# A fifth block product as seven small ones in a mixer's first channel product, with a new order of issue

## The chip, the cores and the metric

The kernel runs on one core of a Trainium2 chip, as one program in one launch. The metric is the device time of that program in microseconds (us); lower is better. Five engines work side by side, each through its own queue in order: TensorE (PE) multiplies, VectorE (DVE) and ScalarE (ACT) do elementwise work, GpSimd (POOL) does a little, and SyncE (SP) issues most transfers. They wait for each other on semaphores. TensorE writes into PSUM[...]; VectorE and ScalarE read those and write SBUF.

## The reference: routed attention, then a token and channel mixer

Four batches of 768 tokens, 512 features, float32:

```
attn = softmax(mask(q k^T / 8)) v                  # 8 heads of 64, keys of the query's cluster only
x    = attn, heads side by side                    # (4, 768, 512)
u    = x + (relu(x^T w_tok1) w_tok2)^T             # token mixing, hidden width 256
out  = u + relu(u w_ch1) w_ch2                     # channel mixing, hidden width 1536
```

The change is in `relu(u w_ch1)`, the first channel product: per batch 768 x 512 times 512 x 1536.

## The kernel before, in words

**Stages.** Attention runs first, then the token mixing of batches 0 and 1 and of 2 and 3, then the channel mixing of batches 0, 2, 3, 1 in that order. Each batch has three parts, so the channel stage has 12. A part makes 512 of the 1536 hidden columns (`ch1_pair`, L784) and uses it at once in the second product (`ch2_chunks`, L960), which adds into the batch's tile `x`.

**Seven products instead of eight.** Both channel products split each operand into 2 x 2 blocks and use Winograd's form of Strassen's scheme: seven block products of sums of blocks, named in `SEVEN` (L545): p1 = A11 B11, p5 = S1 T1, c11 = A12 B21, u2 = S2 T2, c12 = S4 B22, c22 = S3 T3, c21 = A22 T4. The S are sums of weight blocks (the left side), the T sums of blocks of `u` (the right side). A left block of a part is 256 x 256, a right one 256 x 384.

**A second level.** In the first part of batch 0 (`ch1_plain`, L831) all seven are computed as they are, in two chunks of 384 columns each, two matmuls a chunk ("big" products). In the other eleven (`ch1_sets`, L864) four of them, called Y (A12 B21), P (S1 T1), Z (S4 B22) and X (A22 T4), are split once more in the same way, into seven "small" products of 128 x 128 by 128 x 192 each. The rest, A11 B11, S2 T2 and S3 T3, stay big. The left sums of the second level are in the tile `w1ss` (`set_lefts`, L604) and are made once, in batch 0; the right ones, `uTss` (`set_rights`, L620), are made anew for each batch.

**Gathering results.** A small product lies in PSUM, and VectorE adds it (`add`, L566) to the target in SBUF, or ScalarE copies the first one there. Where several partial results accumulate in one bank, the next product may only start when the last state has been read: `chain` (L880) does a small product and the add that reads it. S3 T3 is accumulated in PSUM onto A11 B11 + S2 T2 and VectorE reads the two chunks into `a22`. In the end the hidden blocks pass relu (L810) and VectorE makes the sums S1 to S4 of the second product's left side (L814, L563, L822).

**What sets the order.** The program is written out by hand; no scheduler moves anything. The order of the calls is the order in each queue. Two lists put work between products: `late` holds the rest of a part's gathering and `others` holds weight and right sums; `between` (L740) takes one of each after a big product and after each of the 21 chunks of the second product (`by_turns`, L746). The second product starts with p1, which reads the first hidden block, and reads A12 with c11, in its seventh chunk. In the last part of a batch ScalarE and transfers also turn the next batch's u (`u_steps`, L713), and the right sums for it follow in the first part of the next batch.

**Memory.** The x of batch 1 is written to DRAM after token mixing (`spill`) and read back when batch 0 has left its tile. The tiles for the channel stage reuse the memory of the token stage.

Of the kernel before, what the change touches and what calls it, by code (L numbers as in the profile page):

```python
# [8 lines left out]
F32 = mybir.dt.float32  # L9
# [8 lines left out]
B, H, S, D = 4, 8, 768, 64  # L18
C = 16
# [31 lines left out]
def kernel(  # L51
# [49 lines left out]
    tokpool = pool("tokpool", 1, tokens)  # L101
    staging = fast.enter_context(ExitStack())
# [30 lines left out]
    spill = spilled.tile([P, NJ, DM], F32, name="spill")  # L133
    xs = [(x1pool if b == 1 else xpool).tile([P, NJ, DM], F32, name=f"x{b}") for b in range(B)]
# [466 lines left out]

    def set_lefts():
        if "l2" not in pools:
            pools["l2"] = pools["w2sums"].tile([P, 4, 3, HS], F32, name="w1ss")  # L604
        l2 = pools["l2"]
        yx = W["ch1"].rearrange("p f (i r c) -> p f i r c", i=2, r=2)[:, 2:4]
        pz = pools["w1s"][:, 0:3:2].rearrange("p i f (r c) -> p f i r c", r=2)
        for n, both in enumerate((yx, pz)):
            blocks = [both[:, f, :, r] for r in range(2) for f in range(2)]
            sums_ = [l2[:, 2 * n : 2 * n + 2, m] for m in range(3)]  # L610
            yield dict(
                zip(("A11", "A12", "A21", "A22", "S1", "S2", "S4", "S3"), blocks + sums_ + blocks[2:3])
            )
# [6 lines left out]
    def set_rights():  # L620
        uT, R, r2 = pools["uT"], pools["R"], pools["r2"]
        yz = uT[:, :, 2:4].rearrange("p n f (k t) -> p n f k t", k=2)
        x, p = (R[name].rearrange("p f (k t) -> p f k t", k=2) for name in ("T4", "T1"))
        for blocks, sums_ in (
            ([yz[:, :, f, k] for f in range(2) for k in range(2)], [r2[:, 0:2, m] for m in range(3)]),
            ([x[:, f, k] for f in range(2) for k in range(2)], [r2[:, 2, m] for m in range(3)]),
            ([p[:, f, k] for f in range(2) for k in range(2)], [r2[:, 3, m] for m in range(3)]),
        ):
            yield dict(
                zip(("B11", "B12", "B21", "B22", "T1", "T2", "T4", "T3"), blocks + sums_ + blocks[1:2])  # L630
            )

    def set_right_sums():

        pools["r2"] = pools["w2sums"].tile([P, 4, 3, HS // 2], F32, name="uTss")
        return [list(winograd_right(blocks)) for blocks in set_rights()]

    def set_blocks():

        (yx, pz), (yz, x, p) = (list(y) for y in (set_lefts(), set_rights()))  # L640
        left = {name: {k: a[:, i] for k, a in two.items()} for two, i, name in
                ((yx, 0, "Y"), (yx, 1, "X"), (pz, 0, "P"), (pz, 1, "Z"))}
        right = {"Y": {k: b[:, 0] for k, b in yz.items()}, "Z": {k: b[:, 1] for k, b in yz.items()},
                 "X": x, "P": p}
        return left, right
# [100 lines left out]
    def by_turns(n, product, of, last=False, after=()):  # L746
# [10 lines left out]
        for m in range(len(order) // 2):  # L757
# [9 lines left out]
            between()  # L767
# [16 lines left out]
    def ch1_pair(part, sets, beside):  # L784
# [6 lines left out]
        p5, c12 = (pools["mlp"].tile([P, 2, HS], F32, name=k) for k in ("p5", "c12"))  # L791
# [10 lines left out]

        def big(psum, a, r, i, start):
            product(psum, a, r, i, start)
            between()
            if a != "A11" and beside:
                beside.pop(0)()
# [13 lines left out]
        def sums_34():  # L821
            nc.vector.scalar_tensor_tensor(  # L822
                out=h2["S3"], in0=c12, scalar=0.0, in1=a11, op0=ALU.max, op1=ALU.subtract
            )
            sub(h2["S4"], a12, h2["S2"])

        (ch1_sets if sets else ch1_plain)(
            part, product, big, relu, a11, a12, a22, p5, c12, sum_1, sum_2, sums_34
        )

    def ch1_plain(part, product, big, relu, a11, a12, a22, p5, c12, sum_1, sum_2, sums_34):  # L831
# [24 lines left out]
        def late_(i):  # L856
            product(X[i], "A22", "T4", i, False)
            nc.scalar.activation(out=a12[:, i], in_=X[i], func=ACT.Relu)
            (sums_34 if i else sum_2)()
# [4 lines left out]
    def ch1_sets(part, product, big, relu, a11, a12, a22, p5, c12, sum_1, sum_2, sums_34):  # L864

        left, right = set_blocks()
        n0, n1 = slice(0, HS // 2), slice(HS // 2, HS)

# [7 lines left out]
        def direct(bank, which, start=True):  # L876
            small(bank[:, n0], which, "c11", start)
            small(bank[:, n1], which, "c12", start)

        def chain(q, which, name, x):  # L880

            small(q[:, n0], which, name, name == "p1")
            src = q[:, n0]
            if len(x.shape) == 3:
                src = src.unsqueeze(1).to_broadcast([P, 2, HS // 2])
            add(x, src, x)

        def column(z, which, x):
            small(z[:, n0], which, "p5")
            add(x[:, :, n1], z[:, n0].unsqueeze(1).to_broadcast([P, 2, HS // 2]), x[:, :, n1])  # L890

        X = [ptile("X", HS), None]
        big(X[0], "A11", "B11", 0, True)
        nc.scalar.copy(out=a11[:, 0], in_=X[0])  # L894
        ybe = ptile("Y", HS)
        direct(ybe, "Y")
        add(a11[:, 0], ybe, a11[:, 0])
        X[1] = ptile("X", HS)
        big(X[1], "A11", "B11", 1, True)
        nc.scalar.copy(out=a11[:, 1], in_=X[1])  # L900
        pbe = ptile("Z", HS)
        direct(pbe, "P")
        nc.scalar.copy(out=p5[:, 0], in_=pbe)
        yq, pq = ptile("Y", HS), ptile("Z", HS)
        chain(yq, "Y", "p1", a11[:, 0, n0])
        chain(pq, "P", "p1", p5[:, 0, n0])
        big(X[0], "S2", "T2", 0, False)
        chain(yq, "Y", "u2", a11[:, 0, n1])
        yz, pz = ptile("X", HS), ptile("Z", HS)
        column(yz, "Y", a11)  # L910
        chain(pq, "P", "u2", p5[:, 0, n1])
        small(pz[:, n0], "P", "p5")
        nc.scalar.copy(out=p5[:, 1, n1], in_=pz[:, n0])
        relu(a11[:, 0])
        add(p5[:, 0, n1], pz[:, n0], p5[:, 0, n1])
        add(c12[:, 0], X[0], p5[:, 0])
        big(X[1], "S2", "T2", 1, False)
        chain(yq, "Y", "c22", a11[:, 1, n1])
        chain(pq, "P", "c22", p5[:, 1, n1])
        direct(ybe, "Z")  # L920
        chain(yq, "Y", "c21", a11[:, 1, n0])
        small(pq[:, n0], "P", "c21", False)
        nc.scalar.copy(out=p5[:, 1, n0], in_=pq[:, n0])
        relu(a11[:, 1])
        add(c12[:, 0], ybe, c12[:, 0])
        chain(yz, "Z", "p1", c12[:, 0, n0])
        add(c12[:, 1], X[1], p5[:, 1])
        big(X[0], "S3", "T3", 0, False)
        add(a22[:, 0], X[0], p5[:, 0])
        relu(a22[:, 0])  # L930
        chain(yz, "Z", "u2", c12[:, 0, n1])
        column(pbe, "Z", c12)
        big(X[1], "S3", "T3", 1, False)
        add(a22[:, 1], X[1], p5[:, 1])
        relu(a22[:, 1])
        chain(yz, "Z", "c22", c12[:, 1, n1])
        direct(X[0], "X", False)
        nc.scalar.copy(out=a12[:, 0], in_=X[0])
        small(X[1][:, n0], "X", "c21", False)
        nc.scalar.copy(out=a12[:, 1], in_=X[1])  # L940
        chain(yz, "Z", "c21", c12[:, 1, n0])
        chain(yq, "X", "p1", a12[:, 0, n0])
        sum_1()

        def late_1():
            chain(yq, "X", "u2", a12[:, 0, n1])
            column(pz, "X", a12)
            sum_2()

        def late_2():  # L950
            chain(yq, "X", "c22", a12[:, 1].rearrange("p (k t) -> p k t", k=2))
            relu(a12)
            sums_34()

        late.extend([late_1, late_2])
# [166 lines left out]
    for b in (0, 2):  # L1122
# [26 lines left out]
        if b == 2:  # L1149
            take(turning, len(turning))  # L1150
            usums = u_sums()
            tok2_chunks(b, {13: lambda: next(usums)})
        else:
# [3 lines left out]
            nc.sync.dma_start(spill, xs[1])  # L1157
# [7 lines left out]
    batches = (0, 2, 3, 1)  # L1165
    for n, b in enumerate(batches):
        turning = []
        for part in range(3):
# [8 lines left out]
            ch1_pair(part, not first, [turning.pop(0) for _ in turning[:UCOLS]])  # L1177
# [10 lines left out]
            if part == 2 and not last:  # L1188
                after[3] = lambda: take(turning, len(turning))
# [13 lines left out]
            if part == 2 and not last:  # L1203

                yz, x, p = steps
                yz[0]()
                yz[1]()
                next(usums)

                others += [lambda: next(usums)] * 2  # L1210
                others.append(lambda: [step() for step in (yz[2], p[2], yz[3], p[3])])
                others += [lambda: None, lambda: (x[0](), x[1]()), lambda: (x[2](), x[3]())]
                if n == 0:
                    xs[1] = xpool.tile([P, NJ, DM], F32, name="x0")
                    nc.sync.dma_start(xs[1], spill)
# [216 lines left out]
```

## Time and profile before

Three timed runs gave 823.44 us (823.30 to 823.72). The profiled execution has a span of 821.6 us at a granted TensorE clock of 1.00.

| what | where | us |
|---|---|---|
| channel stage, first product to end | 393.5 to 821.6 | 428 |
| part 0 of batch 0 (all big) | 393.51 to 429.75 | 36.24 |
| part 1 of batch 0 | 429.75 to 465.33 | 35.58 |
| part 2 of batch 0 | 465.33 to 500.41 | 35.08 |
| part 0 of batch 2 | 500.41 to 535.69 | 35.28 |
| part 1 of batch 2 | 535.69 to 570.66 | 34.97 |
| VectorE busy in that part | | 21.73 |
| ScalarE busy in that part | | 5.56 |

The longest groups of VectorE in the channel stage are the adds of the second product into x (128 x 256, 421 ns) and the adds of small products (128 x 192, 355 ns). In the timeline a row is a run of like instructions: start, length, engine, line, output and inputs, shape, count. A float32 matmul is recorded as two instructions, so a big chunk has four and a small product two. Records of TensorE overlap, so the time that a product holds it is the distance from its start to the next one's.

### The profile page before, as it was taken

To read this page: it belongs to the slowest core of one execution; us is meant where nothing else is said; L and a number is where in the kernel's file an instruction comes from. 1 tells how busy PE (TensorE), PEld (TensorE's weight loads), DVE (VectorE), ACT (ScalarE), POOL (GpSimd) and SP (SyncE) were. 2 spreads that over 40 slices of the span, in tenths; PEclk is the share of its full clock that TensorE was granted. 3 is DMA by queue.
4 is the path that set the end of the run, shared out by engine and by line. 5 is a ranking of instruction groups with operands and counts; after the bars stand their busy time and mean duration, and the time that the engine had idled before them with its cause. 6 is when DMAs were issued, how large, how long until landed. Compare 5 with 4: busy or idle time off the path is not lost.

```text
span 821.6 us, 11693 instructions
## 1 busy us (share of the span) xinstructions
PE 814.2 (99%) x4348; PEld 535.5 (65%) x4348; DVE 631.1 (77%) x1206; ACT 374.7 (46%) x573; POOL 30.7 (4%) x28
## 2 busy tenths in 40 slices
PE   8999999999999999999999999999999999999997
PEld 4444444444444444444588888888888888888876
DVE  6879898989898978859797788755777566775665
ACT  5588776777878776127202154121441204511120
POOL 1001010111011000000000000000000000000000
PEclk9999999999999999999999999999999999999999
DMA  8797666768676434143000025000240001400002
GB/s 156 142 162 135 140 142 122 149 139 163 130 160 137 95 104 122 51 127 79 0 1 1 5 45 183 1 0 1 38 117 0 1 1 30 125 1 1 1 0 81
DMA packets 184258, 63.41 MB, mean 77 GB/s; under 512 B 172800, under 2 KB 176896, under 8 KB 183936
## 3 DMA queue, kind: packets, MB, share of 16 engines
q1 hardware_dynamic: 182592, 62.18, 34.7%
q8 instruction: 36, 0.59, 0.3%
q10 hardware_dynamic: 1600, 0.39, 0.2%
q14 instruction: 30, 0.25, 0.1%
HBM read 36.21 MB, written 7.86 MB: 54 GB/s over the span
## 4 chain that ended last, share of the span: by engine, by line
PE 98%; DVE 1%; issue 0%; ACT 0%; DVEq 0%; ACTq 0%
PE sc L413 19%; PE av L455 15%; PE pX L966 15%; PE pX L798 12%; PE pZ L966 7%; PE ph L534 5%; PE pY L871 5%; PE pZ L871 4%; PE pX L871 4%; PE pY L966 4%; PE pX L774 3%; PE small L491 2%; PE pZ L774 1%; PE small L304 1%; PE pZ L798 1%; PE pY L774 1%
## 5 line engine op out<-in xcount | busy, mean ns | idle before, releaser
L437 ACT ACTIVATE ex<-sc 128x768 f32<-128x768 f32 x192 | 151.0, 812 | 27.2 <-PE sc L413 15.5
L413 PE MATMUL sc<-qkT 64*128 64x384 f32 x768 | 155.3, 483 | 0.0
L445 DVE TENSOR_TENSOR sum<-sum,ex 128x768 f32<-128x768 f32 x128 | 127.8, 999 | 27.1 <-ACT ex L437 14.9
L455 PE MATMUL av<-ex,va 128*64 128x384 f32 x768 | 127.4, 488 | 0.0
L566 DVE TENSOR_TENSOR x<-pX,x 128x256 f32<-128x256 f32 (+1 forms) x168 | 75.8, 458 | 38.1 <-PE pX L966 37.6
L455 PEld LDWEIGHTS av<-ex,va 128*64 128x64 f32 x768 | 53.7, 137 | 71.7 <-issue 67.6
L413 PEld LDWEIGHTS sc<-qkT 64*128 64x128 f32 x768 | 67.8, 187 | 38.3 <-issue 38.0
L810 ACT ACTIVATE hA<-hA 128x384 f32<-128x384 f32 (+1 forms) x57 | 34.0, 597 | 85.4 <-DVE hA L566 85.1
L566 DVE TENSOR_TENSOR hA<-pY,hA 128x192 f32<-128x192 f32 (+1 forms) x90 | 36.7, 407 | 45.4 <-PE pY L871 42.7
L798 PE MATMUL pX<-uT,wc 128*128 128x384 f32 x192 | 69.8, 487 | 0.0
L894 ACT COPY hA<-pX 128x384 f32<-128x384 f32 x11 | 5.3, 479 | 131.3 <-PE pX L798 131.3
L413 PE MATMUL sc<-ohT 64*128 64x384 bf16 x384 | 62.4, 323 | 0.0
L462 ACT COPY avrows<-av 128x768 uint16<-128x768 uint16 x32 | 25.5, 797 | 44.4 <-PE av L455 44.4
L566 DVE TENSOR_TENSOR x<-pZ,x 128x256 f32<-128x256 f32 (+1 forms) x84 | 36.4, 455 | 11.4 <-PE pZ L966 11.3
L798 PEld LDWEIGHTS pX<-uT,wc 128*128 128x128 f32 x192 | 35.4, 190 | 14.7 <-issue 0.6
L534 PE MATMUL ph<-x,wt 128*128 128x512 f32 x96 | 41.6, 593 | 0.0
L413 PEld LDWEIGHTS <-ohT 64*128 64x128 bf16 x384 | 18.7, 94 | 33.8 <-issue 9.6
L966 PE MATMUL pX<-wc,hA 128*128 128x256 f32 x144 | 36.9, 380 | 0.3 <-ACT hA L940 0.3
L711 ACT COPY uT<-ucols 128x768 uint16<-128x768 uint16 x32 | 33.2, 1049 | 4.7 <-DMA ucols<-urows 4.7
L966 PE MATMUL pZ<-wc,hS 128*128 128x256 f32 x144 | 35.0, 379 | 0.0
L966 PE MATMUL pY<-wc,hA 128*128 128x256 f32 x144 | 35.0, 379 | 0.0
L798 PE MATMUL pX<-uTs,w1s 128*128 128x384 f32 x96 | 34.9, 486 | 0.0
(189 smaller groups left out, 1310.8 us busy)
## 6 DMA issues: line engine op xcount, KB each, us to landing
raw<-in_moe_w_ch_dram SPq DMA_DIRECT2D x24, 512.0 KB, 4.5
va<-in_v_dram SPq DMA_DIRECT2D x16, 384.0 KB, 3.7
out_dram<-x SPq DMA_DIRECT2D x24, 256.0 KB, 2.3
qk<-in_k_dram SPq DMA_DIRECT2D x60, 96.0 KB, 4.0
qk<-in_q_dram SPq DMA_DIRECT2D x60, 96.0 KB, 3.5
raw<-in_moe_w_tok_dram SPq DMA_DIRECT2D x3, 512.0 KB, 4.1
raw<-in_moe_w_tok_dram SPq DMA_DIRECT2D x4, 384.0 KB, 3.8
spill<-x SPq DMA_DIRECT2D x1, 1536.0 KB, 5.1
```

What stands on the lines that cost most here:

```text
L413: nc.tensor.matmul(sc[:, h, 0:HS], lhsT=src[rows, 1, j], rhs=src[rows, 0, HJ * qh : HJ * qh + HJ], start=start, stop=not start,)
L437: nc.scalar.activation(out=ex, in_=sc[:, :, 0:HS], func=ACT.Exp, scale=SM_SCALE)
L445: nc.vector.tensor_tensor(out=acc, in0=acc if j > 1 else st["ex", qh, 0], in1=st["ex", qh, j], op=ALU.add)
L455: nc.tensor.matmul(av[h * D : (h + 1) * D], lhsT=st["va"][:, h, j], rhs=ex[:, h], start=(j == 0), stop=(j == NJ - 1),)
L534: nc.tensor.matmul(pf, lhsT=W["tok1"][:, j, t * P : (t + 1) * P], rhs=xs[b][:, j], start=(j == 0), stop=(j == NJ - 1),)
L566: nc.vector.tensor_tensor(out=dst, in0=a, in1=b, op=ALU.add)
L711: nc.scalar.copy(out=out, in_=pools.pop(("ucols", i)).rearrange("p w j t -> p w (j t)"))
L774: nc.tensor.matmul(psum, lhsT=A[a][:, i], rhs=R[r], start=start, stop=True, skip_group_check=not start,)
L798: nc.tensor.matmul(psum, lhsT=A[a][:, k, c], rhs=R[r][:, k], start=start and k == 0, stop=k == 1, skip_group_check=not start,)
L810: nc.scalar.activation(out=x, in_=x, func=ACT.Relu)
L871: nc.tensor.matmul(psum, lhsT=left[which][a][:, part * P : part * P + P], rhs=right[which][r], start=start, stop=True, skip_group_check=no ...
L966: nc.tensor.matmul(psum, lhsT=h2[a][:, k, i * P : (i + 1) * P], rhs=Bw[w][:, part + 3 * k], start=start and k == 0, stop=k == 1, skip_grou ...
```

## The change

S3 T3, called U, becomes the fifth block product that is split into seven small ones. It saves an eighth of U's multiplications, and asks for more:

- left sums of U's weights (four more sums of 128 elements per part, `w1ss` grows from four sets to five) and right sums of its u (four of 192 per batch, `uTss` grows likewise);
- a tile `u3` in SBUF for U, which can no longer be accumulated in PSUM onto the rest. The steps V (X + p5), C (c12 + V), B (V + u3) and E (X + u3) gather the hidden blocks from it;
- memory: so the x of batch 3 moves to a pool that is freed after token mixing, is spilled to DRAM like that of batch 1, and both are read back when an earlier batch has left its tile;
- a new order of issue, written as a list of names, `CH1`. A name with a plus is VectorE's add of the small product of that name; a, d, f, g, z and be are p1, u2, c22, c21, p5 and the pair c11, c12 of a block; c0, cz and cg are copies by ScalarE; r11, r22 and r12 are relus; E replaces the copies of X by ScalarE. Bars separate what `between` takes one at a time in the second product. The right sums of a new u (yz, x, p, u with a number, and T2 to T4) stand in the list too, and are taken in the first part of a batch.

In `ch1_sets` no `between` is called any more, so `others` goes on only in the second product, where `by_turns` may now take more than one at a time.

```diff
+    x3pool = pool("x3pool", 1, tokens)
...
+    spill = {b: spilled.tile([P, NJ, DM], F32, name=f"spill{b}") for b in (1, 3)}
+    homes = (xpool, x1pool, xpool, x3pool)
+    xs = [homes[b].tile([P, NJ, DM], F32, name=f"x{b}") for b in range(B)]
...
-            pools["l2"] = pools["w2sums"].tile([P, 4, 3, HS], F32, name="w1ss")
+            pools["l2"] = pools["w2sums"].tile([P, 5, 3, HS], F32, name="w1ss")
...
-        pools["r2"] = pools["w2sums"].tile([P, 4, 3, HS // 2], F32, name="uTss")
+        pools["r2"] = pools["w2sums"].tile([P, 5, 3, HS // 2], F32, name="uTss")
...
-            between()
+            between(-(-len(others) // max(len(order) // 2 - m, 1)))
...
+    BANKS = {
+        "X0": 0, "Zz": 1, "Uz": 1, "Yz": 1, "X1": 2, "Ube": 3, "Pq": 3, "Ybe": 3, "Zq": 4, "Pbe": 5,
+        "Zbe": 5, "Pz": 5, "Yq": 6, "Xz": 6, "Uq": 7, "Xq": 7,
+    }
+    CH1 = """
+        p1_0 yz0 T2 Zz T3 a11_0 p1_1 Zcz yz1 p2 Ube u0 a11_1 u1 p3 Za u2 Uc0 Pbe u3 T4 Pa Pc0 Ya Ua
+        yz2 Zbe +Pa +Ya Pd +Ua Zc0 aside yz3 u2_0 +Pd +Za x0 x1 Ud x2 Pz x3 Zd +Zz Pcz Pf +Ud Uz +Pz
+        V0 u2_1 Ucz aside +Zd +Pf +Uz C0 Zf Yd B0 Yz +Zf Pg r22_0 +Yd Uf +Yz Pcg Zg +Uf Yf V1 Zcg
+        Ybe +Yf Ug C1 Yg +Ybe Ucg Xbe +Yg r11_0 B1 Xa Xg r11_1 E0 Xz r22_1 aside +Xa E1 s1
+        |
+        Xd +Xd s2
+        |
+        +Xz
+        |
+        Xf +Xf
+        |
+        r12 s3
+        |
+        s4
+    """
...
+            do[f"V{i}"] = lambda: add(a22[:, i], X[i], p5[:, i])
+            do[f"C{i}"] = lambda: grow(c12[:, i], a22[:, i])
+            do[f"B{i}"] = lambda: grow(a22[:, i], u3[:, i])
+            do[f"E{i}"] = lambda: add(a12[:, i], X[i], u3[:, i])
...
+        first, *rest = CH1.split("|")
+        issue(first)
+        late.extend([lambda names=names: issue(names) for names in rest])
...
+            nc.sync.dma_start(spill[3], xs[3])
...
-            ch1_pair(part, not first, [turning.pop(0) for _ in turning[:UCOLS]])
+            ch1_pair(part, not first, [turning.pop(0) for _ in turning[:UCOLS]], extra)
...
-                after[3] = lambda: take(turning, len(turning))
+                after[5] = lambda: take(turning, len(turning))
...
-                others += [lambda: next(usums)] * 2
-                others.append(lambda: [step() for step in (yz[2], p[2], yz[3], p[3])])
-                others += [lambda: None, lambda: (x[0](), x[1]()), lambda: (x[2](), x[3]())]
+                for name, sums_ in zip(("yz", "x", "p", "u"), steps):
+                    for m, step in enumerate(sums_):
+                        if name != "p" or m > 1:
+                            extra[f"{name}{m}"] = step
+                for m in (2, 3, 4):
+                    extra[f"T{m}"] = lambda: next(usums)
+                if n < 2:
+                    later = batches[n + 2]
+                    xs[later] = xpool.tile([P, NJ, DM], F32, name=f"x{b}")
+                    nc.sync.dma_start(xs[later], spill[later])
```

## The prediction

> **What bounds the kernel now.** I read the page first.
>
> ```profile
> PE 814.2 (99%) x4348; PEld 535.5 (65%) x4348; DVE 631.1 (77%) x1206; ACT 374.7 (46%) x573; POOL 30.7 (4%) x28
> ...
> PE 98%; DVE 1%; issue 0%; ACT 0%; DVEq 0%; ACTq 0%
> ```
>
> TensorE is busy nearly without pause, and 98% of the chain that ended last is its work. So every product removed is worth its full time, and every wait given to TensorE costs its full time. The question is what the products cost, and whether VectorE still serves them in time. The timeline of TensorE inside one changed part, then that of VectorE, give the prices:
>
> ```profile
> 507.53 1.45 PE L798 MATMUL pX<-uTs,w1s 128*128 128x384 f32 x4
> 508.82 0.49 PE L871 MATMUL pY<-uT,wc 128*128 128x192 f32 x2
> 509.14 0.49 PE L871 MATMUL pZ<-uTs,w1s 128*128 128x192 f32 x2
> ...
> 514.97 0.49 PE L871 MATMUL pX<-uTs,w1ss 128*128 128x192 f32 x2
> 515.50 0.59 PE L871 MATMUL pX<-uTss,wc 128*128 128x192 f32 x2
> 515.93 0.49 PE L871 MATMUL pX<-uTss,w1s 128*128 128x192 f32 x2
> ```
>
> ```profile
> 502.08 0.95 DVE L563 TENSOR_TENSOR uTs<-uT,uTs 128x768 f32<-128x768 f32 x1
> 502.95 0.95 DVE L563 TENSOR_TENSOR uT<-uT 128x768 f32<-128x768 f32 x1
> ...
> 505.15 0.35 DVE L566 TENSOR_TENSOR hA<-pY,hA 128x192 f32<-128x192 f32 x1
> 505.42 0.35 DVE L566 TENSOR_TENSOR p<-pZ,p 128x192 f32<-128x192 f32 x1
> 505.68 0.55 DVE L563 TENSOR_TENSOR uT<-uT 128x384 f32<-128x384 f32 x1
> 506.15 0.35 DVE L563 TENSOR_TENSOR uTs<-uTs 128x192 f32<-128x192 f32 x1
> ...
> 512.31 0.35 DVE L563 TENSOR_TENSOR uTss<-uTs 128x192 f32<-128x192 f32 x1
> 512.69 0.36 DVE L563 TENSOR_TENSOR uTss<-uTs,uTss 128x192 f32<-128x192 f32 x1
> ...
> 514.90 0.55 DVE L566 TENSOR_TENSOR hA<-pX,p 128x384 f32<-128x384 f32 x1
> ```
>
> What counts is start to start. A big chunk product (four records) holds TensorE for 508.82 - 507.53 = 1.29 us, a small one (two records) for 0.32 us (0.3245 over a run of seven). VectorE's next instruction starts 0.27 us after a 192-wide one, 0.47 after a 384-wide, 0.87 after a 768-wide; likewise 0.33 after 256 and 0.60 after 512. An instruction that needs the result of the one just before it on VectorE starts about 0.13 us later still (0.38 at 512.31). TensorE went on 0.05 us after the recorded end of the add that it waited for (514.90 + 0.55, then 515.50); that wait was 0.21 us, and the product after it took 0.11 us too long, so each wait costs 0.11 us on top. A product can be read 0.52 us after its small start. In the windows of the parts, one without waits takes 34.97 us, the one at 500.41 takes 35.28. In all 12 parts the gaps between TensorE's starts sum to about 2.2 us, so little is to be won back there.
>
> **What the Trainium skill says.** VectorE: DVE Perf Modes, section on the TRN2 errata, gives a float32 add as (N + 151)/0.96 ns: 357, 557 and 957 for 192, 384 and 768. The trace agrees (352 to 355, 550, 950); its starts are some 0.08 us closer, since neighbours overlap. The same page, Rules for kernel authors, says to minimize the count of operations, not semaphores: four narrow adds pay that fixed part four times; the 0.13 us above shows that a wait is not quite free. TensorE: Matmul & The Clock Gate, section LDWEIGHTS, says a load's time goes with its columns, whatever the product's width, so narrow products could become bound by loads. The trace says no: loads take 190 ns a record, overlap, and 192-wide products still run at half the time of 384-wide ones. Perfetto Trace Analysis, Tensor Engine Instruction, says that ends of matmuls are estimated; hence starts here.
>
> **The change, part by part.** Eleven of twelve parts use the new list.
>
> *Products.* Two S3 T3 chunks (2.58 us) become seven small products (2.27): -0.31 us a part, all on the bound, -3.4 us in all. A part without a wait would take 34.67 us.
>
> *VectorE.* Per part before: 14 adds of 192, 10 of 384 and 4 of 768 (3.78 + 4.70 + 3.48 = 12.0 us). After: 18 of 192 and 12 of 384, the same 768 (14.0 us). Four more accumulate u; B and E (a22 + u3, and X + u3 in place of two ACT copies) are 384-wide; two adds of Z became ACT copies. With 21 adds of 256 (6.9 us), VectorE has 20.9 us in 34.7. So the sum fits easily; the order decides. I walk the queues with the prices above; time runs from the start of p1_0, names are those of the list.
>
> *Ordinary part, first wait.* TensorE reaches Pz after 3 big and 13 small products: 3.87 + 4.22 = 8.09. Its copy Pcz can start at 8.61 and is seen at 8.98 (ACT copies 192 in 0.32). +Pz writes the same tile and stands behind it. From there VectorE has no pause: +Pz 0.40 with the wait of V0 on it, V0 0.47, +Zd +Pf +Uz 0.81, C0 0.61 (B0 waits), B0 0.47, +Zf 0.27, +Yd 0.43 (+Yz waits), +Yz 0.47, +Uf 0.27, V1 0.50. So +Yf starts at 13.68 and is seen 0.41 later, at 14.09. Yg accumulates onto the bank that +Yf reads. TensorE gets to Yg after 4 big and 27 small products: 5.16 + 8.76 = 13.92. Wait 0.17 + 0.11. Queued behind Yg: everything.
>
> *Ordinary part, second wait.* The list's tail is spread over five turns of the second product where the old one took two (relu r12 in the fourth, before in the second), and an add of x stands between each. From +Yf at 13.69: C1 +Ybe +Yg B1 E0 +Xa E1 take 3.39 to s1 at 17.08; then s1, x, +Xd, s2, x, +Xz, x bring +Xf to 20.58 (0.87 + 0.33 + 0.27 + 0.87 + 0.33 + 0.47 + 0.36). It is seen at 21.18, and relu r12 (0.84) at 22.07. c11 chunk 0 reads it; TensorE comes there at 16.52 (4 big, 35 small) + 6 x 0.865 + 0.28 = 21.99. Wait 0.08 + 0.11. The part takes 34.67 + 0.47 = 35.14 against 34.98: +0.16, in five parts +0.8.
>
> *First part of a batch* (three). The right sums of the new u now include four of U, and all stand early in the list: from 0.20 VectorE has the last x add 0.33, yz0 0.47, T2 and T3 1.77, yz1 0.47, the six p2 u0 u1 p3 u2 u3 1.76, T4 1.00, yz2 0.50. So +Pa starts at 6.50 and is seen at 6.90; Pd, which accumulates onto the same bank, is reached after 2 big and 11 small products, 6.15. Wait 0.75. VectorE stays late: further waits of 0.01 at Uz, 0.06 at Zg, 0.21 at Yg, 0.20 at c11. With four restarts: 1.23 + 0.44 = 1.67. The old part lost 0.30. Each is 1.67 - 0.31 - 0.30 = +1.06 (the first some 0.1 less): +3.1.
>
> *Batch 0, parts 1 and 2.* Here weight sums of 0.60 and 0.33 us stand in the turns too. With +Xf in the third turn, two of them stand ahead of it: 1.2 us in part 1, 0.66 in part 2, so c11 waits 1.28 + 0.11 and 0.74 + 0.11. With Yg's 0.28, less 0.31, and less the old wait of 0.30 in part 1 (none in part 2): +1.06 and +0.82, together +1.9.
>
> *Last part:* the old lost 0.6, also around the register load at 796.77, which stays; the same waits as above and one of Zf's kind in the last order give about +0.3.
>
> *Spill of x3, reloads.* The old copy of x1 landed in 5.1 to 7.0 us. x3's last row is written at about 392.1 (L566 adds of L774's products), so its copy lands by 399.2; the first write over it is the second stage's w1ss sum, at 401.35 in the old trace. Slack 2 us: nothing. From the other side: a copy twice as slow would hold VectorE 5 us, TensorE perhaps 3. I take nothing. The reloads have a batch's time each: nothing.
>
> Sum: 0.8 + 3.1 + 1.9 + 0.3 = +6.1, so 829.5 us. The same walk through the old list gives 34.98 and 35.28 for parts that measure 34.97 and 35.28, and meets VectorE's starts within 0.15 us; that is why I trust it over the page's shares.
>
> **The rivals.** *No waits:* VectorE is ahead, as its 77% and the 60% per part would suggest; then -3.4 and up to 1.5 us of old waits also vanish: 818.5 to 820. Against it: +Yf's slack is -0.17 us by the walk, and the first parts miss by 0.75, far over the 0.15 of error. *Cancelling:* waits only half as long, each some 0.15 us shorter, no restart cost: 822 to 825. *The copy of x3 or banks hold more:* 831.5 to 834, if the copy lands late or each of about 28 waits is 0.1 us longer.
>
> **How the numbers follow.** Forecast 0.74, no waits 0.08, cancelling 0.09, longer 0.09. About 28 waits, each uncertain by 0.1 us, give 2.8 us either way; without the restart cost 3 less. Both at once reach 823.7, above I stop at 832: range 824.8 to 832. Faster 0.10, same 0.06, slower 0.84 (half of the cancelling case ends above 825.1).
>
> **What would show it.** Seven small products of u at 0.3245 us each: the saving is right. Gaps of TensorE before Yg in every changed part, before Pd in three, before c11 chunk 0 behind ACT's relu, largest in batch 0 parts 1 and 2; parts of about 35.1, 36.3, 36.5 and 35.8 us. If parts take 34.7 instead, VectorE's prices or the waits that I read into the list are wrong, and so is the forecast. A gap at 401 in the first part would be the copy.

## The result and the profile after

The changed kernel took 825.98 us (median of six runs, 825.52 to 826.63), the kernel before 823.37 (six runs beside them, 822.86 to 823.72). The ratio is 1.0032, with a 95% interval of 1.0019 to 1.0045. So the change makes the kernel slower by 2.6 us. The forecast of 829.5 us had the direction; of the +6.1 us that it added, less than half came.

The page of the changed kernel answers to the two lines of before like this:

```profile
PE 815.1 (99%) x4414; PEld 542.7 (66%) x4414; DVE 650.5 (79%) x1300; ACT 388.3 (47%) x617; POOL 30.7 (4%) x28
...
PE 95%; DVE 4%; issue 1%; ACT 0%; DVEq 0%; ACTq 0%
```

TensorE is busy for 99% of the span in both, and its busy time even grows by 0.9 us, although it does less work. The page's first part shows nothing of the loss. The chain does: VectorE's share rises from 1% to 4%, which means that the end now runs back through adds that TensorE waits for. The Trainium skill (Perfetto Trace Analysis, Identifying the Most-Contended Engine) says that a matmul's busy share is no good measure of how close a kernel is to its roofline, since pipelined instructions look smaller in the trace. Here too the share tells nothing, though the records look larger, not smaller: they overlap, and a small product is recorded with 0.49 us where it holds TensorE for 0.32. The kernel before, the changed one and the seven of the experiments all show 99%, over times from 819.9 to 828.9 us.

Waits are read better at the weight loads, which stand ahead of each product. First the kernel before, then the changed one, in the channel stage (us in total, number of waits, longest):

```profile
PEld pX L871 <- DVE hA L566: 1.0, 3, 0.3
...
PEld pX L966 <- ACT hA L940: 0.6, 1, 0.6
PEld pX L966 <- DVE x L566: 0.5, 1, 0.5
...
PEld pY L871 <- DVE hA L566: 0.2, 1, 0.2
```

```profile
PEld pY L993 <- ACT hA L818: 4.0, 10, 1.4
PEld pY L916 <- DVE hA L568: 2.7, 11, 0.3
PEld pZ L916 <- DVE p L568: 1.9, 3, 0.7
PEld pZ L916 <- issue: 1.5, 3, 0.5
PEld pX L916 <- DVE uTss L565: 0.9, 3, 0.3
PEld pX L993 <- ACT hA L818: 0.8, 1, 0.8
```

These are the places that the forecast named: c11 chunk 0 behind ACT's relu r12 (ten times), Yg behind +Yf (eleven), Pd behind +Pa (three). Two rows are new to it, both in the first parts of batches. The three waits marked "issue" stand before Ube, the first small product of U: the profile names no releaser, but Ube reads T3, which ends at 504.95 us in the first of these parts, and its load starts at 505.07. The three waits on `uTss` (L565) stand before Zz, and cost TensorE nothing, since the load is still early enough there.

Weight loads run ahead of their products, so a load's wait is longer than what TensorE loses. What it loses is the distance from one product's start to the next, less 0.3225, 0.2161 and 0.1622 us a record of 384, 256 and 192 columns. Summed over the stage, these gaps grow from 2.2 to 8.5 us; eleven parts save 0.31 us each (8 records of 384 against 14 of 192), 3.4 us. The difference, 2.9 us, is what the channel stage grew by, counted here and below from the start of its first product to the start of its last: 423.04 us before, 425.95 after. The profiled spans differ by 3.3 us; the other 0.34 us lies ahead of the attention's first product, in the start of the program, and differs from run to run.

The lengths of the parts in us, before and after, beside the forecast:

| part | before | after | difference | forecast |
|---|---|---|---|---|
| part 1 of batch 0 | 35.59 | 36.35 | +0.76 | +1.06 |
| part 2 of batch 0 | 35.07 | 35.70 | +0.63 | +0.82 |
| first part of batches 2, 3, 1 | 35.28, 35.41, 35.28 | 35.88 each | +0.60, +0.47, +0.60 | +1.06 each |
| five ordinary parts | 34.97 | 34.93 | -0.04 each | +0.16 each |
| last part | 35.32 | 35.37 | +0.05 | +0.3 |

Two windows of the changed kernel, an ordinary part and the first part of batch 2 (length, then busy time of PE, PEld, DVE, ACT, POOL with the number of records):

```profile
502.13:538.01 35.88, 35.50 (x171) 30.06 (x170) 29.81 (x72) 6.81 (x16) 0.00 (x0) 1.00 0.19 71
538.01:572.94 34.93, 34.93 (x172) 30.27 (x170) 22.74 (x55) 6.81 (x16) 0.00 (x0) 1.00 0.00 1
```

VectorE is busy for 22.7 us of 34.9 in the ordinary part, 65%, and yet it is late twice in it. The timeline of the ordinary part at the first of these places:

```profile
551.16 0.55 DVE L568 TENSOR_TENSOR hA<-pX,p 128x384 f32<-128x384 f32 x1
...
551.62 1.00 PE L916 MATMUL pY<-uTss,wc 128*128 128x192 f32 x4
551.62 0.35 DVE L568 TENSOR_TENSOR hA<-pY,hA 128x192 f32<-128x192 f32 x1
...
552.03 0.30 PEld L916 LDWEIGHTS pY<-uTss,wc 128*128 128x128 f32 x2 [0.21 <-DVE hA L568]
...
552.46 0.33 PE L916 MATMUL pX<-uTs,wc 128*128 128x192 f32 x1
```

The add at 551.62 is +Yf. The four records of TensorE at 551.62 are Ug and Yg; Yg's load can start only at 552.03, just after +Yf ends at 551.97. The next product, Xbe, starts 0.84 us after Ug, where two small products take 0.65: 0.19 us are lost, 0.08 before Yg and 0.105 inside it. The row at 551.16 is V1, which stands ahead of +Yf on VectorE and has no haste.

And the second place, c11 chunk 0:

```profile
558.99 0.84 ACT L818 ACTIVATE hA<-hA 128x768 f32<-128x768 f32 x1 [4.70 <-DVE hA L568]
...
559.88 1.59 PEld L993 LDWEIGHTS pY<-wc,hA 128*128 128x128 f32 x8 [0.21 <-ACT hA L818]
```

The relu of A12 had been waiting 4.70 us for VectorE's add +Xf. It ends at 559.83, and the load of c11 starts 0.05 us later. Here TensorE lost only 0.078 us, all of it inside c11's first product.

The copy of x3 to DRAM was issued at 392.5 us and landed 5.0 us later; the first write over the tile is at 401.68, 0.59 us after the start of the 128 x 512 subtraction ahead of it on VectorE, which is back to back. So nothing waited for this copy.

### The profile page after: what moved, and what is told of

Read it like the earlier page. It is cut to its first block, busy times and chain, and to the rows that moved or that the text cites. A ratio compares the mean times of both kernels' runs of the same rounds, so it can differ in the third digit from the quotient of the medians.

```text
span 824.9 us, 11958 instructions
## 1 busy us (share of the span) xinstructions
PE 815.1 (99%) x4414; PEld 542.7 (66%) x4414; DVE 650.5 (79%) x1300; ACT 388.3 (47%) x617; POOL 30.7 (4%) x28
## 4 chain that ended last, share of the span: by engine, by line
PE 95%; DVE 4%; issue 1%; ACT 0%; DVEq 0%; ACTq 0%
PE sc L415 19%; PE av L457 15%; PE pX L993 15%; PE pX L802 7%; PE pZ L993 7%; PE pZ L916 6%; PE ph L536 5%; PE pY L916 5%; PE pY L993 4%; PE pX L778 3%; PE pX L916 2%; PE small L493 2%; PE pZ L778 1%; PE small L306 1%; DVE hA L568 1%; DVE uTss L565 1%
## 5 line engine op out<-in xcount | busy, mean ns | idle before, releaser
L958 ACT COPY hA<-pX 128x384 f32<-128x384 f32 x22 | 10.5, 479 | 133.2 <-PE pX L802 133.2
L818 ACT ACTIVATE hA<-hA 128x384 f32<-128x384 f32 (+1 forms) x57 | 31.6, 590 | 81.0 <-DVE hA L568 81.0
L568 DVE TENSOR_TENSOR p<-pZ,p 128x192 f32<-128x192 f32 x44 | 15.6, 354 | 41.7 <-ACT p L944 34.7
L568 DVE TENSOR_TENSOR x<-pZ,x 128x256 f32<-128x256 f32 (+1 forms) x84 | 38.4, 463 | 11.3 <-PE pZ L993 11.1
L802 PE MATMUL pX<-uT,wc 128*128 128x384 f32 x104 | 37.8, 487 | 0.0
L993 PE MATMUL pY<-wc,hA 128*128 128x256 f32 x144 | 35.8, 385 | 1.5 <-ACT hA L818 1.5
L993 PE MATMUL pX<-wc,hA 128*128 128x256 f32 x144 | 35.1, 380 | 0.5 <-ACT hA L818 0.5
L802 PE MATMUL pX<-uTs,w1s 128*128 128x384 f32 x96 | 34.9, 486 | 0.0
```

What stands on the lines that cost most here:

```text
L568: nc.vector.tensor_tensor(out=dst, in0=a, in1=b, op=ALU.add)
L802: nc.tensor.matmul(psum, lhsT=A[a][:, k, c], rhs=R[r][:, k], start=start and k == 0, stop=k == 1, skip_group_check=not start,)
L818: nc.scalar.activation(out=x, in_=x, func=ACT.Relu)
L993: nc.tensor.matmul(psum, lhsT=h2[a][:, k, i * P : (i + 1) * P], rhs=Bw[w][:, part + 3 * k], start=start and k == 0, stop=k == 1, skip_grou ...
```

## The experiments

The theory at this point was that VectorE's order costs the time: three waits, each of which can be taken away by changing what stands ahead of one instruction. The rival was the memory: the spill and the two reloads. Times are medians; the kernel before took 823.17 us beside the first four kernels below, and 823.08 beside the other three, which ran on another chip. Each is compared with the kernel before on its own chip. All of them compute the whole reference.

**+Yf ahead of V1.** V1 and C1 move behind the adds for which TensorE waits.

```diff
-        ... +Uf Yf V1 Zcg
-        Ybe +Yf Ug C1 Yg +Ybe Ucg ...
+        ... +Uf Yf Zcg
+        Ybe +Yf V1 Ug Yg +Ybe C1 Ucg ...
```

> The changed kernel with +Yf moved ahead of V1 on VectorE, and C1 behind +Ybe. Theory (the time went into single waits of TensorE on VectorE's queue): the wait before Yg, 0.19 us in eight parts and 0.30 in three, vanishes. But r12 comes no sooner, since VectorE's queue up to it is as long as before, so the wait before the first c11 chunk grows by what Yg gave back: ordinary parts stay at 34.9 us, 825.5 to 826.3 in all. Rival A (each wait costs by itself): 11 times about 0.2 us, 823.5. Rival B (small products cost more than half a big one, no wait matters): 826.0 with Yg's products still late.

Measured: 826.44 us (825.78 to 826.96), ratio 1.0040 (1.0026 to 1.0053), just above what was expected. The ordinary part takes 34.95 us, no less than the 34.93 without the swap. Its waits in the channel stage:

```profile
PEld pY L993 <- ACT hA L818: 6.1, 10, 1.6
PEld pZ L916 <- DVE p L568: 1.9, 3, 0.6
...
PEld pY L916 <- DVE hA L568: 0.6, 3, 0.2
```

The wait before Yg is gone from all parts (the three left in this row stand before Xd, behind +Xa, in the first parts of batches), and the one before c11 has taken its place: 4.0 became 6.1 us of the loads. In TensorE's starts c11 now loses 0.18 + 0.104 us where it lost 0.078. The relu's time had not moved, so TensorE only came to it earlier. Two waits that stand one behind the other are not two costs that add: the first was hiding most of the second.

**Relu earlier.** In the third turn of the second product, +Xf and the relu r12 now stand ahead of S2.

```diff
-        Xd +Xd s2
+        Xd +Xd
         |
         +Xz
         |
-        Xf +Xf
+        Xf +Xf r12 s2
         |
-        r12 s3
+        s3
```

> The changed kernel with r12 moved ahead of S2, into the third turn of the second product, so that relu of A12 starts one 768-wide sum (0.87 us) sooner. Theory: the waits before c11, 1.28 us in batch 0 part 1 and 0.75 in part 2, shrink to about 0.4 and 0; the 0.08 in the others goes. Parts 35.6, 34.9, 35.7 and 34.85; saves about 2.2 to 3.2 us, 822.8 to 823.8. Rival A (VectorE's total work sets the time): unchanged, 826. Rival B (spill and reload of x): unchanged, 826.

Measured: 823.82 us (823.34 to 824.57), ratio 1.0010 (1.0004 to 1.0017). The channel stage takes 423.88 us, 2.07 less than in the changed kernel. The waits now:

```profile
PEld pY L916 <- DVE hA L568: 2.7, 11, 0.3
PEld pZ L916 <- DVE p L568: 1.9, 3, 0.7
...
PEld pY L993 <- ACT hA L818: 0.5, 1, 0.5
```

c11 waits once, in part 1 of batch 0 (0.31 + 0.104 us, where it was 1.18 + 0.104), and not at all in part 2; the ordinary part takes 34.85 us, 0.08 less. In part 1 a quarter of the gain is lost again to a later chunk of the second product, which waits 0.12 + 0.104 us for an add into x. So the order S2 before +Xf cost 2.1 us, 1.4 of it in the two parts of batch 0 where weight sums stand in the same turns.

**Right sums in the part before.** T2 and T3 of a new u (two subtractions of 0.87 us) move from the head of the first part into turns 16 and 18 of the part before, where two smaller sums, p0 and p1, make room.

```diff
-        p1_0 yz0 T2 Zz T3 a11_0 p1_1 Zcz yz1 p2 Ube ...
+        p1_0 yz0 Zz p0 a11_0 p1_1 Zcz p1 yz1 p2 Ube ...
...
-                after[17] = lambda: (steps[2][0](), steps[2][1]())
+                after[16] = lambda: next(usums)
+                after[18] = lambda: next(usums)
...
-                        if name != "p" or m > 1:
+                        if True:
...
-                for m in (2, 3, 4):
+                for m in (4,):
```

> The changed kernel with the right sums T2 and T3 of the new u made in the last turns of the part before, where VectorE has 0.5 us free a turn, and the two small sums of P in their place. Same work, nothing left out. Theory: the wait before Pd (0.62 us) and the ones behind it in the first part of three batches go; those parts fall from 35.88 to about 34.95; saves 2.6 to 2.9 us, 823.1 to 823.5. Rival A (VectorE's total work sets the time, wherever it stands): 826. Rival B (the added sums only push the turns before late): the first parts gain 0.9 and the parts before them lose as much, 826.

Measured: 823.55 us (823.02 to 823.82), ratio 1.0004 (0.9996 to 1.0013), no difference from the kernel before. The row of Pd is gone from the waits, and the first part of batch 2 is as long as an ordinary one:

```profile
PEld pY L993 <- ACT hA L818: 4.0, 10, 1.4
PEld pY L916 <- DVE hA L568: 2.4, 11, 0.2
PEld pX L916 <- DVE uTss L565: 1.4, 3, 0.6
```

```profile
501.77:536.70 34.93, 34.93 (x172) 30.23 (x171) 29.02 (x73) 6.81 (x16) 0.00 (x0) 1.00 0.20 73
```

VectorE does as much in this part as before (29.0 us against 29.8), only not ahead of +Pa. The other two first parts take 35.19 and 35.12 us, because Zz, the second product of the list, now waits 0.15 and 0.09 us (and 0.105 each) for its right sum. The stage takes 423.57 us, 2.38 less than in the changed kernel.

**The spill alone.** The kernel before, with only the memory part of the change: x3 in its own pool, spilled, and both x read back one batch ahead.

```diff
+    x3pool = pool("x3pool", 1, tokens)
...
+    spill = {b: spilled.tile([P, NJ, DM], F32, name=f"spill{b}") for b in (1, 3)}
+    homes = (xpool, x1pool, xpool, x3pool)
+    xs = [homes[b].tile([P, NJ, DM], F32, name=f"x{b}") for b in range(B)]
...
+            nc.sync.dma_start(spill[3], xs[3])
...
+                if n < 2:
+                    later = batches[n + 2]
+                    xs[later] = xpool.tile([P, NJ, DM], F32, name=f"x{b}")
+                    nc.sync.dma_start(xs[later], spill[later])
```

> The kernel before with one edit: x of batch 3 in a pool of its own, spilled and read back as in the changed kernel. Theory: nothing of the 2.6 us comes from it, 823.4 within 0.6. Rival (memory): transfers and reused tiles cost 1 us or more, 824.5 to 826, with a gap of VectorE in the first part of batch 0.

Measured: 823.05 us (822.74 to 823.48), ratio 0.9998 (0.9990 to 1.0006). The parts are as long as in the kernel before, to 0.02 us. The memory costs nothing, and the rival falls.

**One more add.** If the price of VectorE's queue is what sets the wait before Yg, one more add of 128 x 192 ahead of +Yf must lengthen it by the add's full spacing, though VectorE has 12 us free in the part. The add writes into the tile of S3, which is written over later, so nothing that is computed changes.

```diff
-        Ybe +Yf Ug C1 Yg ...
+        Ybe load +Yf Ug C1 Yg ...
...
+        self_s3 = pools["h2"]["S3"]
+        load = lambda: add(self_s3[:, 0, n0], a22[:, 0, n0], a22[:, 0, n1])
```

> The changed kernel with one more add of 192 elements on VectorE, right ahead of +Yf, in all eleven parts; its result is written over later, so it is pure load. Theory: there VectorE has no slack, so the wait before Yg grows by the add's 0.265 us and all behind it moves along: parts of 35.19 and 36.14 us, 828.4 to 829.1. Rival (VectorE, busy 60% of a part, takes it into its idle time): 826.0.

Measured: 828.92 us (828.57 to 830.07), ratio 1.0074 (1.0060 to 1.0087). The wait before Yg grows by 0.27 us in each of the eleven parts (from 0.08 to 0.35 in an ordinary one, from 0.19 to 0.46 in a first part), and the parts by 0.27 each (35.20 for an ordinary one); the rows of the waits, whose lines have moved by two:

```profile
PEld pY L918 <- DVE hA L568: 5.6, 11, 0.6
PEld pY L995 <- ACT hA L818: 4.0, 10, 1.4
```

The wait before c11 stays, since VectorE and TensorE are both late by the same 0.27 us there. This is the slope that the forecast needed: at this place an error in VectorE's price goes into the time one for one, eleven times. The Trainium skill (VectorE: DVE Perf Modes, Rules for kernel authors) says to minimize the count of VectorE's operations; the trace agrees where the operation stands in the queue ahead of an awaited one. The third experiment shows that elsewhere it can be free: in part 2 of batch 0, which makes T2 and T3 for batch 2, VectorE is busy for 28.1 us instead of 27.4, and the part takes 35.71 us where it took 35.70.

**The swap and the early relu together.**

```diff
-        ... Zg +Uf Yf V1 Zcg
-        Ybe +Yf Ug C1 Yg +Ybe Ucg ...
+        ... Zg +Uf Yf Zcg
+        Ybe +Yf V1 Ug Yg +Ybe C1 Ucg ...
...
-        Xd +Xd s2
+        Xd +Xd
...
-        Xf +Xf
+        Xf +Xf r12 s2
...
-        r12 s3
+        s3
```

> The changed kernel with +Yf ahead of V1 and r12 ahead of S2, without the third move. Theory: the first move gave nothing alone since c11 took the wait over; with r12 early it must give 0.19 us in each ordinary part: 34.67 us there, 35.5 in first parts, and 1.7 to 2.0 us less than with r12 alone: 821.8 to 822.2. Rival (the first move is worth nothing in itself): 823.8, as with r12 alone.

Measured: 822.56 us (821.95 to 822.82), ratio 0.9993 (0.9985 to 1.0002), somewhat above the expected time. The ordinary part takes 34.66 us: no gap is left in it, and it is 0.18 shorter than with the early relu alone. The stage goes from 423.88 to 422.56 us. So the swap, worth nothing alone, is worth 1.3 us once the wait behind it is gone. It falls short of the expected 1.7 to 2.0 because parts 1 and 2 of batch 0 gain nothing: they take 35.72 and 35.14 us, where they took 35.70 and 34.96 with the early relu alone. In part 1 the wait before c11 grows from 0.31 to 0.52, and in part 2 Xd now waits 0.16 us for +Xa. The first parts take 35.58 us, 0.92 over the ordinary one: 0.84 of it lies in the first 10 us, at Ube, Pd and Uz, behind T2 and T3 in VectorE's queue.

**All three.** Swap, early relu and the right sums in the part before; the diff is that of the last experiment and that of the third together.

> The changed kernel with the three moves of the first experiments together: +Yf ahead of V1, r12 ahead of S2, and T2 and T3 in the part before. Same work. Theory: with no wait left ahead of Yg, c11 and Pd, ordinary parts show the products alone, 34.67 us (0.30 less than the kernel before), the first parts of batches 34.7 to 34.95; about 1.6 us of wait remain in batch 0 part 1 and the last part. 819.6 to 820.6, faster than both kernels. Rival (small products cost more, or VectorE's total work sets the time): 822.5 or more, with parts of 34.9.

Measured: 819.94 us (819.73 to 820.12), ratio 0.9962 (0.9948 to 0.9976): faster than the kernel before by 3.1 us, and than the changed one, whose interval (1.0019 to 1.0045) lies wholly above. The stage takes 419.77 us. The window of an ordinary part, and the place of Yg in it:

```profile
535.19:569.86 34.67, 34.67 (x172) 30.30 (x170) 22.77 (x55) 6.92 (x16) 0.00 (x0) 1.00 0.00 1
```

```profile
548.35 0.36 DVE L568 TENSOR_TENSOR hA<-pY,hA 128x192 f32<-128x192 f32 x1
...
548.63 0.55 DVE L568 TENSOR_TENSOR hA<-pX,p 128x384 f32<-128x384 f32 x1
...
548.80 0.81 PE L916 MATMUL pY<-uTss,wc 128*128 128x192 f32 x4
...
549.45 0.49 PE L916 MATMUL pX<-uTs,wc 128*128 128x192 f32 x2
```

+Yf (548.35) now stands ahead of V1 (548.63) and ends before Yg's turn; Ug and Yg take 549.45 - 548.80 = 0.65 us. VectorE's busy time in the part is the same as in the changed kernel (22.77 against 22.74). From batch 2 on all eight parts ahead of the last take 34.66 or 34.67 us: the saving of 0.31 us a part is there in full, once the order lets it through. The waits that still cost TensorE time lie in batch 0 and ahead of the last part's second product, the longest of them:

```profile
PEld pY L993 <- ACT hA L818: 1.0, 2, 0.8
PEld pX L993 <- ACT hA L818: 1.0, 1, 1.0
```

TensorE's gaps in the stage sum to 2.3 us, where the kernel before had 2.2, so the removed multiplications and these waits account for the whole stage. Put one on top of the other, the moves bring 2.07 us (early relu), 1.32 (swap) and 2.79 (right sums), together 6.18 = 425.95 - 419.77. Each alone, they bring 2.07, -0.17 and 2.38, together 4.28: waits that stand one behind the other don't add.

## Why the prediction was right in its direction and wrong in its size

- **Products: right.** Forecast -0.31 us a part, measured -0.31 in the records, and 34.97 against 34.67 in the kernel without waits.
- **Places of the waits: right, all but one.** Yg behind +Yf, Pd behind +Pa, c11 behind the relu, largest in parts 1 and 2 of batch 0. Each was taken away by an experiment, and with all three moves the time came back. Unforeseen was Ube, which loses 0.07 + 0.076 us in the first parts and no longer does when T2 and T3 are made before; it makes TensorE come to Pd 0.145 us later, and so shortens the wait there. The restart (what the product that waited takes longer) was about as long as the forecast's 0.11 us: 0.104 or 0.105 at Yg, at Pd and at c11 in batch 0, but 0.075 to 0.079 at Ube, Uz and c11 in the other parts.
- **Spill and reloads: right.** Nothing, shown by the kernel with the spill alone.
- **Sizes of the waits: here it failed.** The waits came where the walk of the two queues had put them, but about two thirds as long. The steps "Ordinary part, first wait", "second wait" and "First part of a batch" put the waits too long, always in the same direction:

| wait, without restart | forecast | measured |
|---|---|---|
| Yg, ordinary part | 0.17 | 0.08 |
| c11, ordinary part | 0.08 | none to be seen |
| Pd, first part of a batch | 0.75 | 0.52 |
| all others there, with Ube | 0.48 | 0.26 |
| c11, part 1 and part 2 of batch 0 | 1.28 and 0.74 | 1.18 and 0.65 |

Over five ordinary parts that is 5 x 0.17 = 0.85 us, over three first parts 3 x 0.45 = 1.35, over the two of batch 0 about 0.4 (Yg is in them too). Of the 3.2 us by which the stage's +2.9 fell short of +6.1, that is 2.6; 0.2 are shorter restarts at c11 and 0.25 the last part. Most of the rest is old waits that the forecast took too short: it subtracted 0.30 us each for part 1 of batch 0 and for the first part of batch 3, where the kernel before lost 0.40 and 0.44.

The waits are too long because the walk prices VectorE's queue too long. A wait here is the end of a long queue on VectorE less the end of a long queue on TensorE, a small difference of two large numbers. Set beside the trace, +Yf starts 13.61 us into the ordinary part (walk: 13.68), +Xf at 20.39 (20.58), and +Pa 6.41 us into the first part of batch 2 (6.50). From +Pz to +Yf the walk has 4.70 us, the trace 551.62 - 546.98 = 4.64:

```profile
546.98 0.36 DVE L568 TENSOR_TENSOR p<-pZ,p 128x192 f32<-128x192 f32 x1 [0.32 <-ACT p L945]
...
548.64 0.55 DVE L568 TENSOR_TENSOR c<-hA,c 128x384 f32<-128x384 f32 x1
549.23 0.56 DVE L568 TENSOR_TENSOR hA<-u,hA 128x384 f32<-128x384 f32 x1
```

The eight steps that the walk priced plainly, at 0.27 or 0.47 us, are together only 0.013 us shorter in the trace. The four to which it added something for a wait of one instruction on another are 0.045 shorter. From C0 (548.64) to B0 (549.23), for example, the walk has 0.61 us and the trace 0.585, and from V1 to +Yf (551.16 and 551.62, shown above) it has 0.50 and the trace 0.464, a plain spacing. The same holds in the first part: the plain steps ahead of +Pa agree, and those with an addition (T2 and T3 at 1.77 us, measured 1.74; six sums at 1.76, measured 1.74; T4 and yz2) hold the whole 0.09. The forecast's own line at 512.31 gives 0.38 - 0.27 = 0.11 us for such a wait, where the walk used 0.13 and more; and the 0.03 that it added at V1, at T2 and T3, at yz2 and at the last add into x before +Xf is not read from any line it shows.

TensorE has a part in it too. It came to Yg 0.015 us later than the walk had it, and to Pd 0.15 later because of Ube. At c11 in an ordinary part it came 0.09 us earlier, since less was lost at Yg; but the relu was ready 0.2 us earlier. The added add shows what such errors cost: at +Yf, 0.27 us more in the queue were 0.27 us more of wait in each of eleven parts. So 0.07 us there count eleven times. The range took the errors of 28 waits as 0.1 us each with one sign, 2.8 us in all; they did have one sign, and 2.6 us of it came. That the time still lies inside the range rests on this width and not on the sizes of the waits.

The rival "cancelling" had the better number, but only half of its mechanism: the waits were shorter, but its "no restart cost" did not come. It stood at 0.09, though the walk's error (within 0.15 us) was about as large as the wait of 0.17 on which the ordinary part hung. What the forecast should have done is to check each addition for a wait against a place in the trace of before, and to give all waits a common error instead of trusting each one's size.

Two numbers of the forecast don't follow from its own lines. Its signs have 36.5 and 35.8 us for parts 1 and 2 of batch 0, while its terms give 35.58 + 1.06 = 36.64 and 35.08 + 0.82 = 35.90. And of the 5.1 to 7.0 us that it gives to the old copy of x1, only 5.1 is the copy; 7.0 is the read back.

What stays open is where the 0.31 us come from that the early relu leaves at c11 in part 1 of batch 0. Weight sums stand in the same turns, and the changed `by_turns` may take more than one of them at a time; neither was varied in any run.

## What to carry to other kernels

When the bound engine waits for a helper engine, don't ask how busy the helper is, ask what stands ahead of each awaited instruction in its queue: here a helper at 65% cost 6 us of waits, and moving five of its instructions out of the way of awaited ones brought 6.2 us back with the same work. Where two waits stand close one behind the other, take the later one away first: removing the earlier one alone (Yg) only made TensorE come sooner to the next, while a wait with none close behind it (Pd) gave its time back at once. And when a forecast hangs on the small difference of two long queues, check every step of the longer one against the trace, the additions for waits above all: a few hundredths of a us, all of one sign, made waits half as long again here.

## What the runs showed of the hardware that was not expected

- A wait costs TensorE more than its length, since the product that waited also takes longer. In most places this was 0.104 to 0.105 us, after 0.03 us of wait (first part of batch 3 in the kernel before) as after 1.18 us (c11 in part 1 of batch 0 in the changed one). But it was 0.075 to 0.079 us at Uz and c11 in the changed kernel, where no wait ahead of the product is to be seen, and also after 0.07 us at Ube and after 0.66 us at the start of the second product of the last part. No run shows what decides between the two.
- One added add of 0.35 us duration moved the end of each part by 0.27 us, its spacing, not by its duration.
- VectorE's spacing without pauses is the same within 5 ns whether an instruction reads PSUM or SBUF alone: medians of 0.264 and 0.269 us at 192 columns, 0.465 and 0.466 at 384. After a pause of VectorE the spacing is longer: 0.275 and 0.475 us.
